# Chunked attention and a maxout layer on one core: units of 6, 8, 8 and 6 tiles, later transposes at the turn of two units, and another order of the free banks

## The chip, the cores and the metric

The kernel runs on one core of a Trainium2 chip. The metric is the device time of one execution in microseconds (us); the median of several runs counts.

## The reference

Attention inside chunks of 64 positions for 8 batches and 8 heads, then a layer that takes the largest of three products and projects it:

```python
scores = scale * np.matmul(q_c, k_c.transpose(0, 1, 2, 4, 3))     # chunks of 64 positions, heads of 64
scores = scores - np.max(scores, axis=-1, keepdims=True)
attn = np.exp(scores)
attn = attn / (np.sum(attn, axis=-1, keepdims=True) + 1e-09)
out = np.matmul(attn, v_c)
...
x = np.ascontiguousarray(attn_out.transpose(0, 2, 1, 3)).reshape(B * S, H * D)     # 4608 x 512
h = np.maximum(np.maximum(x @ w1, x @ w2), x @ w3)                                 # 4608 x 768
return (h @ w_out).astype(np.float32)                                              # 4608 x 512
```

## The kernel before, in words

The 4608 positions are 36 tiles of 128. The first eight tiles are two groups of four; the other 28 are four *units*, before of 8, 8, 6 and 6 tiles (`UNITS`, L27). A product of fp32 numbers is made of three matmuls on a high and a low part (`three`, L188 to L191), so nearly all of PE's work has the lines L189, L190 and L191.

*First group* (`first_group`, L642): an order written out by hand (`FIRST`, L49). It splits the weights into high and low parts, computes the attention of tiles 0 to 7 and the layer for tiles 0 to 3. Its last steps are the four output tiles, copied out of their banks at L360.

*Group 1* (tiles 4 to 7): its hidden part, 18 products of four steps each, and its projection (`project`, L364). Between the steps stand the attention steps of the first unit's tiles, one tile at a time (`tiles`, L703), and the sums of weights that the units need (`store`, L384), which go to DRAM.

*Units*: a unit's hidden part is nine *sets* of seven products (`hidden`, L490), a scheme that forms sums of weight blocks and of `X` blocks so that seven products do the work of eight; a product takes two steps of three matmuls, 512 columns wide in a unit of eight tiles and 384 in one of six. The weights of a set come from DRAM in two loads, 0.79 and 1.05 MB, into one of two buffers (`ring`, L471). After its nine sets a unit's tiles are projected (`project`, L574): the first four of six blocks for tiles 0 to 2, then the other two for them, then tile by tile; a tile's sum stays in one bank until ACT has copied it out (L564). While a unit is projected, the `X` operands of the next unit are made of `stage` (`operands`, L465: casts on ACT at L459, subtractions on DVE at L454 and L463, two of them on POOL).

*Attention of a tile* (`plain_steps`, L219): S, the scores (L239), in one half of the two banks of `s`; mx and sub, maximum and subtraction on DVE (L244, L249); exp on ACT (L253); sum, eps, rec on DVE (L197, L200, L203); nrm, the norm (L206); T, four transposes on PE (L262) into `tp`; at, the copy of `tp` on ACT (L267); V, the value product (L278); x, the copy into `stage` on ACT (L292 for single tiles, L726 for pairs). For the first unit's tiles V writes the other half of the same two banks of `s`. The tiles of later units are taken in pairs while the unit before runs: an *insertion* (`insertion`, L730) computes V of one pair, in two banks taken from the common ones, and S of the next, and plans the other steps of that next pair behind it.

The order is that of a planner: `plan(at, pe, fn)` puts a step on a list with a due time, and `passed(step)` (L666) advances the planned time by each PE step and issues what has come due, on whichever engine. Within an engine this order is the order of execution. `TABLE`, `PAIR` and `PAIR_T` (L32 to L37) hold the due times, `series` (L751) spreads a unit's insertions over its hidden part, the last one 3.5 us of planned time before its end.

Five banks serve all products of group 1 and the units. `take` hands out the first of a list, `give` puts a bank back at its end. In the first group a bank goes to the end of the list as soon as it is taken (`kept_until_read` is false), so group 1 begins with the banks in the order in which they were last taken.

Of the kernel before, what the change touches and what calls it, by code (L numbers as in the profile page):

```python
# [23 lines left out]
CT, JT = DM // P, DF // P  # L24
SCALE = 1.0 / float(D) ** 0.5
GROUPS = [4, 4]
UNITS = [8, 8, 6, 6]  # L27
HALF = 512
STEP, TILE = 0.6815, 2.05
STEP_H = {6: 0.517, 7: 0.6003, 8: 0.6815}  # L30
# [37 lines left out]
def chunk_attn_maxout_kernel(  # L68
# [27 lines left out]
    ps_m = ctx.enter_context(tc.tile_pool(name="ps_m", bufs=1, space=PSUM))  # L96
# [2 lines left out]
    first_x = tc.tile_pool(name="ps_x", bufs=1, space=PSUM)  # L99
    ps["ps_x"] = first_x.__enter__()  # L100

    banks, kept_until_read = [(ps_m, f"pm{n}") for n in range(3)], False

    def take():
        assert banks, "no bank is free"
        pool, tag = place = banks.pop(0)
        if not kept_until_read:
            banks.append(place)
        return pool.tile([P, 512], F32, name="pm", tag=tag), place

    def give(place):
        assert kept_until_read
        banks.append(place)
# [15 lines left out]
    for name in FIRST.split():  # L129
        k = (3 * int(name[1]) + int(name[2])) if name[0] in "WAXY" else None  # L130
# [57 lines left out]
    def three(o, ah, al, bh, bl, first, last):  # L188
        nc.tensor.matmul(out=o, lhsT=al, rhs=bh, start=first, stop=False)  # L189
        nc.tensor.matmul(out=o, lhsT=ah, rhs=bl, start=False, stop=False)  # L190
        nc.tensor.matmul(out=o, lhsT=ah, rhs=bh, start=False, stop=last)  # L191
# [117 lines left out]
    def moe(t0, x_of, first=False):  # L309


        hh, hl = [None] * JT, [None] * JT
        banks, ps, at = {}, {}, {}

        def bank(key):
            ps[key], at[key] = take()

        def read(key):
            if not first:
                give(at[key])  # L320


        def products(j, w, lo, hi):
            n, cols = hi - lo, slice(lo, hi)
            xh, xl = x_of()
            bank((j, w, lo))
            for ct in range(CT):
                three(ps[j, w, lo][:, :n], wh[j][:, w, ct, :], wl[j][:, w, ct, :], xh[:, ct, cols], xl[:, ct, cols],
                      ct == 0, ct == CT - 1)
                yield  # L330

        def maximum(j, w, lo, hi):
            n = hi - lo
            if w == 0:
                banks[j] = mp.tile([P, 512], F32, name="m")
                nc.scalar.copy(out=banks[j][:, :n], in_=ps[j, w, lo][:, :n])
            else:
                nc.vector.tensor_tensor(out=banks[j][:, :n], in0=ps[j, w, lo][:, :n], in1=banks[j][:, :n], op=ALU.max)
            read((j, w, lo))

        def high(j, lo, hi):
            if hh[j] is None:
                both = hpool.tile([P, 2, 512], F32R, name="h", tag=f"h{j}")
                hh[j], hl[j] = both[:, 0], both[:, 1]
            nc.scalar.copy(out=hh[j][:, lo:hi], in_=banks[j][:, :hi - lo])

        def low(j, lo, hi, eng=nc.vector):
            eng.tensor_tensor(out=hl[j][:, lo:hi], in0=banks[j][:, :hi - lo], in1=hh[j][:, lo:hi].bitcast(F32),
                              op=ALU.subtract)

        def onto(tt, j):
            if j == 0:
                bank(tt)
            cols = slice(tt * P, (tt + 1) * P)
            three(ps[tt], hh[j][:, cols], hl[j][:, cols], woh[:, j, :], wol[:, j, :], j == 0, j == JT - 1)

        def output(tt):
            outputs.append(tt)
            o = ao_p.tile([P, DO], F32, name="ao", tag=f"ao{len(outputs) % 4}")
            nc.scalar.copy(out=o, in_=ps[tt])  # L360
            read(tt)
            nc.sync.dma_start(out=out[(t0 + tt) * P:(t0 + tt + 1) * P, :], in_=o)

        def project(*tts, before=JT - 1):  # L364

            for js in (range(before), range(before, JT)):
                for tt in tts:
                    for j in js:
                        onto(tt, j)
                        yield [(0.3, lambda tt=tt: output(tt))] if j == JT - 1 else []  # L370

        def hidden(j, w):
            for ct, _ in enumerate(products(j, w, 0, 512)):
                yield [] if ct < CT - 1 else [(0.3, lambda: maximum(j, w, 0, 512))] + (
                [(1.1, lambda: high(j, 0, 512)), (1.8, lambda: low(j, 0, 512))] if w == 2 else [])

        return dict(products=products, maximum=maximum, high=high, low=low, hidden=hidden, project=project,
                    onto=onto, output=output)
# [295 lines left out]
    def plan(at, pe, fn):  # L674
        heapq.heappush(due, (at, len(order), pe, fn))
        order.append(fn)
# [21 lines left out]
    units, t0 = [], sum(GROUPS)  # L698
    for count in UNITS:
        units.append((unit(t0, count, rooms), t0, count))  # L700
        t0 += count

    def tiles(lead, time):  # L703
        _, t0, count = units[0]
        for tt in range(count):
            first = now + lead + (time - 13.5 - lead) * tt / (count - 1)
            for at, pe, fn in attention(t0 + tt, stage, tt * P, nc.vector, LATER):
                plan(first + at, pe, fn)
# [8 lines left out]
    def value_banks(both):  # L717
        def fn():
            both["banks"] = [take() for _ in range(2)]
            both["x"] = [p.rearrange("p (s g x) -> p s g x", s=2, g=4) for p, _ in both["banks"]]  # L720
        return fn

    def staged(both, c):
        def fn():
            to = stage()[:, :, both["col"]:both["col"] + 2 * P].rearrange("p g (s c x) -> p c s g x", s=2, c=2)
            nc.scalar.copy(out=to[:, c], in_=both["x"][c])  # L726
            give(both["banks"][c][1])
        return fn

    def insertion(when, k):  # L730

        scored = pairs[k]["tiles"] if k < len(pairs) else []
        if k:
            plan(when, 0.0, value_banks(pairs[k - 1]))
            for n, steps in enumerate(pairs[k - 1]["tiles"]):
                plan(when + 0.001 * (n + 1), 0.5, steps["V"])
                plan(when + 1.2 + 0.6 * n, 0.0, staged(pairs[k - 1], n))
        lead = 1.0 * bool(k)
        for n, steps in enumerate(scored):
            plan(when + 0.003 + 0.001 * n, 0.65, steps["S"])  # L740
            for name, *at in PAIR:
                fn = steps[name]
                plan(when + lead + at[n], 0.0, (lambda fn=fn: fn(nc.gpsimd)) if name == "nrm" else fn)
            for name, *at, pe in PAIR_T:
                plan(when + lead + at[n], pe, steps[name])
            plan(when + 6.0 + n, 0.0, steps["v"])
        if k + 1 < len(pairs):
            for n, steps in enumerate(pairs[k + 1]["tiles"]):
                plan(when + 4.0 + n, 0.0, steps["q"])

    def series(u, time):  # L751

        done = sum(count // 2 for _, _, count in units[1:u + 1])
        if u + 1 >= len(units):
            return
        n = units[u + 1][2] // 2
        lead = 9.0
        if u == 0:
            for m, steps in enumerate(pairs[0]["tiles"]):
                plan(now - 4.0 + m, 0.0, steps["q"])  # L760
            plan_at = now + 4.0
            insertion(plan_at, 0)
            lead = 20.0
        for k in range(n):
            insertion(now + lead + (time - 3.5 - lead) * k / (n - 1), done + k + 1)

    def stores():
        for n in range(len(sets)):
# [19 lines left out]

    inner = 3 * JT * CT * STEP + UNITS[0] * TILE
    parts += [("do", lambda: tiles(7.0, inner - 2.0))]  # L790
# [3 lines left out]
    def units_of(u):  # L794
        return UNITS[u] if u < len(UNITS) else 0

    for u, (it, t0, count) in enumerate(units):
        time = len(sets) * 14 * STEP_H[count] + (units_of(u + 1) * 1.6)
# [7 lines left out]
    now = -10.0  # L806
# [6 lines left out]
    with tc.manual_schedule(engines={ET.PE, ET.DVE, ET.Activation, ET.Pool, ET.SP}):  # L813
        first_group()
        kept_until_read = True
        for what, make in parts:
            if what == "do":
                make()
                continue
            for after in make():  # L820
                step, after = after if isinstance(after, tuple) else (STEP, after)
                for at, fn in after:
                    plan(now + step + at, 0.0, fn)
                passed(step)
        while due:
            heapq.heappop(due)[3]()
# [31 lines left out]
```

## Time and profile before

| | us |
|---|---|
| median of 3 runs (lowest, highest) | 670.89 (669.76, 671.49) |
| the profiled execution | 669.72 |
| its span, first to last instruction | 667.7 |
| busy in it: PE matmuls | 631.5 |
| PE weight loads | 536.1 |
| DVE | 416.1 |
| ACT | 233.4 |
| POOL | 210.5 |
| mean granted clock of TensorE | 0.985 of full |

PE's matmuls run one behind another; its weight loads lie beside them. An engine works through its own instructions in order, and an instruction that waits holds up all behind it on that engine. The profile names for each wait the instruction that ended it; "issue" stands where it names none. Times in the rows below are counted from the first instruction.

### The profile page before, as it was taken

The page shows a single profiled execution, that of the slowest core. Times are in us where ns is not written, and L with a number is a line of the kernel's source. Part 1 is how long each engine was busy: PE and PEld are TensorE (multiplying, and loading weights), DVE is VectorE, ACT ScalarE, POOL GpSimd, SP SyncE. Part 2 cuts the span into 40 slices and gives each one's busy share as a digit, 9 for nine tenths or more (in the row PEclk, how much of TensorE's full clock was granted, in tenths as well). Part 3 has the DMA queues.
Part 4 walks back from the last instruction along what each step waited for, and adds up shares of the span by engine and source line. Part 5 has one row for each costly group of instructions (what it writes and reads, how often), then busy time and mean ns, then how long its engine had stood idle before and what let it go on. Part 6 is the DMA issues. An engine that isn't in the chain of part 4 may idle for free.

```text
span 667.7 us, 12398 instructions
## 1 busy us (share of the span) xinstructions
PE 631.5 (95%) x5102; PEld 536.1 (80%) x5102; DVE 416.1 (62%) x663; ACT 233.4 (35%) x400; POOL 210.5 (32%) x184
## 2 busy tenths in 40 slices
PE   8899999787999999995999999969999999999997
PEld 4778868566788888884888888847999998999986
DVE  5889845576576967779027685790176867275640
ACT  5887633243442423244122223232132424121221
POOL 3324476563034232415012341340132322123210
PEclk9999999898999999997999999998999999999999
DMA  8979557364475756625217465162186636276502
GB/s 331 379 254 335 180 211 285 125 236 178 160 255 200 303 219 221 206 100 216 94 55 293 170 257 214 45 278 80 48 316 231 243 130 254 77 273 245 221 10 86
DMA packets 36055, 133.70 MB, mean 200 GB/s; under 512 B 4000, under 2 KB 6560, under 8 KB 30240
## 3 DMA queue, kind: packets, MB, share of 16 engines
q1 hardware_dynamic: 35856, 132.79, 53.9%
q8 instruction: 40, 0.66, 0.4%
q10 hardware_dynamic: 144, 0.13, 0.1%
q14 instruction: 15, 0.12, 0.1%
HBM read 106.95 MB, written 25.95 MB: 199 GB/s over the span
## 4 chain that ended last, share of the span: by engine, by line
PE 82%; DVE 10%; issue 2%; ACT 2%; POOL 2%; DMA 1%; SPq 0%; POOLq 0%; DVEq 0%; ACTq 0%
PE pm L189 25%; PE pm L190 25%; PE pm L191 25%; PE tp L262 2%; PE s L239 2%; PE pm L278 1%; DVE kept L454 1%; DVE X L463 1%; PE s L278 1%; DVE e L249 1%; DVE mx L244 1%; POOL kept L454 1%; DVE sm L197 1%; DVE H L533 1%; DMA buf<-in_qk 1%
## 5 line engine op out<-in xcount | busy, mean ns | idle before, releaser
L189 PE MATMUL pm<-X,ring 128*128 128x512 f32 (+1 forms) x504 | 185.0, 367 | 0.0
L190 PE MATMUL pm<-X,ring 128*128 128x512 f32 (+1 forms) x504 | 182.5, 362 | 0.0
L191 PE MATMUL pm<-X,ring 128*128 128x512 f32 (+1 forms) x504 | 182.5, 362 | 0.0
L511 DVE TENSOR_TENSOR kept<-pm,kept 128x512 f32<-128x512 f32 (+1 forms) x72 | 44.7, 621 | 122.9 <-PE pm L191 122.7
L517 POOL TENSOR_TENSOR kept<-kept 128x512 f32<-128x512 f32 (+1 forms) x36 | 41.4, 1151 | 246.4 <-DVE kept L511 233.2
L189 PEld LDWEIGHTS pm<-X,ring 128*128 128x128 f32 x504 | 94.6, 188 | 10.2 <-DVE pm L514 0.3
L191 PEld LDWEIGHTS pm<-X,ring 128*128 128x128 f32 x504 | 94.6, 188 | 10.2
L190 PEld LDWEIGHTS pm<-X,ring 128*128 128x128 f32 x504 | 94.7, 188 | 9.3
L508 ACT COPY kept<-pm 128x512 f32<-128x512 f32 (+1 forms) x72 | 38.4, 533 | 140.3 <-PE pm L191 134.8
L189 PE MATMUL pm<-woh,H 128*128 128x512 f32 x168 | 67.7, 403 | 0.0
L190 PE MATMUL pm<-wol,H 128*128 128x512 f32 x168 | 66.9, 398 | 0.0
L191 PE MATMUL pm<-woh,H 128*128 128x512 f32 x168 | 66.8, 398 | 0.0
L189 PE MATMUL pm<-xh,wl 128*128 128x512 f32 (+1 forms) x156 | 62.2, 399 | 1.7 <-ACT ao L360 1.7
L190 PE MATMUL pm<-xl,wh 128*128 128x512 f32 (+1 forms) x156 | 59.5, 381 | 0.3 <-DVE xl L289 0.3
L191 PE MATMUL pm<-xh,wh 128*128 128x512 f32 (+1 forms) x156 | 59.3, 380 | 0.0
L514 DVE TENSOR_TENSOR pm<-pm,kept 128x512 f32<-128x512 f32 (+1 forms) x72 | 45.3, 629 | 13.2 <-PE pm L191 12.6
L206 POOL TENSOR_TENSOR e<-e,sm 128x512 f32<-128x512 f32 x25 | 27.8, 1112 | 71.4 <-DVE sm L203 62.2
L523 DVE TENSOR_TENSOR most<-pm,most 128x512 f32<-128x512 f32 (+1 forms) x72 | 44.9, 623 | 2.1
L529 ACT CAST H<-most 128x512 fp32r<-128x512 f32 (+1 forms) x48 | 27.0, 569 | 37.9 <-DVE most L523 37.9
L244 DVE TENSOR_REDUCE mx<-s 128x8 f32<-128x512 f32 x36 | 24.6, 684 | 22.6 <-PE s L239 22.6
L262 PE MATMUL tp<-ident,e 128*128 128x128 f32 x144 | 23.0, 284 | 16.3 <-ACT xs L267 12.3
L189 PEld LDWEIGHTS pm<-woh,H 128*128 128x128 f32 x168 | 32.7, 195 | 6.8
(94 smaller groups left out, 961.7 us busy)
## 6 DMA issues: line engine op xcount, KB each, us to landing
ring<-w SPq DMA_DIRECT2D x36, 1024.0 KB, 6.7
ring<-w SPq DMA_DIRECT2D x36, 768.0 KB, 4.5
buf<-in_qk SPq DMA_DIRECT2D x36, 512.0 KB, 6.0
buf<-in_vb SPq DMA_DIRECT2D x36, 256.0 KB, 6.2
w<-s SPq DMA_DIRECT2D x9, 1024.0 KB, 5.1
out_x<-ao SPq DMA_DIRECT2D x35, 256.0 KB, 2.0
stage<-in_w SPq DMA_DIRECT2D x7, 512.0 KB, 5.4
xl<-in_w SPq DMA_DIRECT2D x5, 512.0 KB, 7.7
```

The lines of the kernel that those rows point to most:

```text
L189: nc.tensor.matmul(out=o, lhsT=al, rhs=bh, start=first, stop=False)
L190: nc.tensor.matmul(out=o, lhsT=ah, rhs=bl, start=False, stop=False)
L191: nc.tensor.matmul(out=o, lhsT=ah, rhs=bh, start=False, stop=last)
L206: eng.tensor_tensor(out=e, in0=e, in1=sm.unsqueeze(2).broadcast_to([P, 8, 64]), op=ALU.mult)
L244: nc.vector.tensor_reduce(out=st["mx"].rearrange("p (g c) -> p c g", c=2), in_=st["s"], axis=AX.X, op=ALU.max)
L262: nc.tensor.transpose(out=tp[:, g, :], in_=st["e"][:, g].rearrange("p c k -> p (c k)"), identity=ident)
L508: return lambda: nc.scalar.copy(out=kept(k), in_=o[i])
L511: return lambda: nc.vector.tensor_tensor(out=kept(k), in0=o[i], in1=kept(q), op=plus)
L514: return lambda: nc.vector.tensor_tensor(out=o[i] if w else M(j, c), in0=o[i], in1=kept(k), op=plus)
L517: nc.gpsimd.tensor_tensor(out=kept(2), in0=kept(2), in1=kept(1), op=plus)
L523: return lambda: nc.vector.tensor_tensor(out=M(j, c), in0=of(), in1=M(j, c), op=most)
L529: nc.scalar.copy(out=hh[j][:, c * half:(c + 1) * half], in_=M(j, c))
```

## The change

The units become 6, 8, 8 and 6 tiles. So six instead of eight single tiles stand in group 1, and 11 instead of 10 pairs in the units. `insertion` gets a time `behind`, by which the transposes of the pair that it scores, and their copies, stand later: 14 us of planned time for the last insertion of a unit's hidden part, 0 for the others. In the last but one unit the last insertion scores no pair. When the first group is done, the list of free banks is sorted by the place of each bank's last reading in the first group.

```diff
-UNITS = [8, 8, 6, 6]
+UNITS = [6, 8, 8, 6]
...
-    banks, kept_until_read = [(ps_m, f"pm{n}") for n in range(3)], False
+    banks, kept_until_read, read_last = [(ps_m, f"pm{n}") for n in range(3)], False, []
...
         def read(key):
-            if not first:
+            if first:
+                read_last.append(at[key])
+            else:
                 give(at[key])
...
-    def insertion(when, k):
+    def insertion(when, k, behind=0.0):
...
             for name, *at, pe in PAIR_T:
-                plan(when + lead + at[n], pe, steps[name])
+                plan(when + lead + behind + at[n], pe, steps[name])
...
         for k in range(n):
-            insertion(now + lead + (time - 3.5 - lead) * k / (n - 1), done + k + 1)
+            insertion(now + lead + (time - 3.5 - lead) * k / (n - 1), done + k + 1, 14.0 if k == n - 1 else 0.0)
...
         kept_until_read = True
+        banks.sort(key=lambda place: max(n for n, other in enumerate(read_last) if other == place))
```

What it moves, at two places. The first is PE's order in the hidden part of group 1. Before, one piece of it (`s<-buf` are the scores of a tile, `s<-xs,buf` the value product of the tile two ahead, `pm<-xh,wl` and the like the products of group 1):

```order
L190 MATMUL pm<-xl,wh_116 128x512
L191 MATMUL pm<-xh,wh_116 128x512
L239 MATMUL s<-buf 64x64 x16
L278 MATMUL s<-xs,buf 64x64 x16
L189 MATMUL pm<-xh,wl_122 128x512
L190 MATMUL pm<-xl,wh_116 128x512
```

and now:

```order
L278 MATMUL s<-xs,buf 64x64 x16
L189 MATMUL pm<-xh,wl_123 128x512
L190 MATMUL pm<-xl,wh_117 128x512
L191 MATMUL pm<-xh,wh_117 128x512
L189 MATMUL pm<-xh,wl_123 128x512
L190 MATMUL pm<-xl,wh_117 128x512
L191 MATMUL pm<-xh,wh_117 128x512
L239 MATMUL s<-buf 64x64 x16
L189 MATMUL pm<-xh,wl_123 128x512
L190 MATMUL pm<-xl,wh_117 128x512
L191 MATMUL pm<-xh,wh_117 128x512
```

Scores and value product no longer stand side by side: six matmuls of group 1 lie between a value product and the next scores, and 18 more, with a transpose after the first three, between those scores and the next value product.

The second is the projection of unit 0 on ACT. Before (`X` are the casts of the next unit's operands, `xs<-tp` the copies out of the transposes, `ao<-pm` the output tiles):

```order
L459 CAST X6_2135<-kept_2107 128x1024
L459 CAST X3_2141<-stage_1531 128x1024
L267 COPY xs_3385<-tp_3375 128x512
L459 CAST X7_2151<-stage_1531 128x1024
L459 CAST X4_2167<-kept_2107 128x1024
L267 COPY xs_3404<-tp_3395 128x512
L564 COPY ao_3413<-pm_3301 128x512
L564 COPY ao_3422<-pm_3344 128x512
```

and now:

```order
L461 CAST X3_2033<-stage_1512 128x1024
L461 CAST X7_2043<-stage_1512 128x1024
L461 CAST X4_2059<-kept_1999 128x1024
L566 COPY ao_3291<-pm_3193 128x512
L566 COPY ao_3300<-pm_3236 128x512
L566 COPY ao_3310<-pm_3261 128x512
L566 COPY ao_3332<-pm_3306 128x512
L566 COPY ao_3355<-pm_3328 128x512
L267 COPY xs_3362<-tp_3350 128x512
L267 COPY xs_3378<-tp_3370 128x512
L566 COPY ao_3390<-pm_3358 128x512
```

The two copies stood among the casts and now stand behind the outputs of five of the unit's six tiles; on PE the two transposes moved from behind the 9th and the 12th step of the projection to behind the 30th and the 33rd.

## Rows read from the trace of the kernel before

**Rows 1.** The page: busy time of PE; GB/s moved in 40 slices of the span.

```profile
PE 631.5 (95%) x5102; PEld 536.1 (80%) x5102; DVE 416.1 (62%) x663; ACT 233.4 (35%) x400; POOL 210.5 (32%) x184
GB/s 331 379 254 335 180 211 285 125 236 178 160 255 200 303 219 221 206 100 216 94 55 293 170 257 214 45 278 80 48 316 231 243 130 254 77 273 245 221 10 86
```

**Rows 2.** PE's waits, whole span: who waited for whom, us, times, longest.

```profile
PE s L278 <- issue: 8.4, 5, 3.0
...
PE s L278 <- ACT s L412: 2.6, 1, 2.6
PE pm L189 <- ACT ao L360: 1.7, 1, 1.7
```

**Rows 3.** Stretches: us, busy PE, PEld, DVE, ACT, POOL, clock, DMA share, GB/s.

```profile
97.95:177.68 79.73, 68.72 (x760) 54.32 (x761) 48.38 (x72) 27.73 (x43) 38.17 (x41) 0.96 0.55 197
...
294.48:338.37 43.89, 36.34 (x153) 29.50 (x152) 23.83 (x25) 14.69 (x21) 9.15 (x4) 0.92 0.42 162
...
432.60:475.76 43.16, 36.37 (x159) 29.48 (x153) 18.84 (x24) 12.87 (x21) 8.10 (x4) 0.92 0.40 161
475.76:549.21 73.45, 73.42 (x716) 71.83 (x714) 48.92 (x96) 20.32 (x40) 22.16 (x22) 1.00 0.57 209
549.21:573.86 24.65, 24.65 (x114) 20.37 (x109) 13.91 (x15) 10.39 (x17) 4.72 (x2) 1.00 0.52 202
573.86:639.41 65.55, 65.55 (x380) 65.54 (x378) 38.92 (x74) 13.64 (x28) 18.13 (x18) 1.00 0.54 201
```

**Rows 4.** The same view of four stretches at half clock.

```profile
121.75:124.90 3.15, 3.15 (x37) 2.65 (x38) 0.79 (x2) 1.11 (x2) 1.64 (x2) 0.50 0.29 83
155.40:159.00 3.60, 3.60 (x16) 2.80 (x10) 3.31 (x6) 1.70 (x3) 1.42 (x2) 0.53 0.50 182
311.02:316.10 5.08, 5.08 (x14) 4.20 (x15) 5.08 (x4) 1.85 (x3) 3.28 (x1) 0.50 0.02 3
451.26:456.00 4.74, 4.74 (x14) 3.87 (x15) 0.36 (x1) 2.00 (x4) 0.00 (x0) 0.50 0.29 111
```

**Rows 5.** Timelines of DVE, PE and ACT in group 1: start, us, instruction.

```profile
154.00 0.68 DVE L244 TENSOR_REDUCE mx<-s 128x8 f32<-128x512 f32 x1
...
154.79 0.69 PE L278 MATMUL s<-xs,buf 64*64 64x64 f32 x32 [2.60 <-ACT s L412]
...
163.35 0.69 PE L278 MATMUL s<-xs,buf 64*64 64x64 f32 x32 [0.87 <-issue]
...
175.56 0.69 PE L278 MATMUL s<-xs,buf 64*64 64x64 f32 x32
...
176.32 0.59 ACT L292 COPY stage<-s 128x512 f32<-128x512 f32 x1 [2.84 <-PE s L278]
```

**Rows 6.** PE's waits from 290 to 470 us, the two projections.

```profile
PE tp L262 <- ACT xs L267: 12.3, 2, 6.6
PE tp L262 <- POOL e L206: 2.0, 2, 1.1
```

**Rows 7.** ACT's timeline in the projections of units 0 and 1.

```profile
310.30 0.58 ACT L267 COPY xs<-tp 128x512 f32<-128x512 f32 x1
...
315.06 1.04 ACT L459 CAST X<-kept 128x1024 fp32r<-128x1024 f32 x1 [3.23 <-POOL kept L454]
...
449.80 0.83 ACT L459 CAST X<-kept 128x768 fp32r<-128x768 f32 x1 [3.63 <-POOL kept L454]
```

**Rows 8.** DVE: one row of unit 0's projection; two groups by shape (count, busy us, mean ns).

```profile
305.04 0.68 DVE L533 TENSOR_TENSOR H<-most,H 128x512 fp32r<-128x512 f32 x1
...
L523 DVE TENSOR_TENSOR most<-pm,most 128x512 f32<-128x512 f32 x36 | 24.9, 690 | 1.0
...
L523 DVE TENSOR_TENSOR most<-pm,most 128x384 f32<-128x384 f32 x36 | 20.0, 556 | 1.1
```

**Rows 9.** The chain that ended last, in group 1: start, us, what.

```profile
169.53 0.62 PE s L278 x32
```

**Rows 10.** DMA issued at 493.14: KB, us from issue to landing.

```profile
ring<-w SPq DMA_DIRECT2D x1, 1024.0 KB, 8.2
```

## The prediction

> **What bounds the kernel now.** I read the page's busy times first, then PE's list of waits, then the span cut into the program's stages, and last the timelines around each wait. PE works for 631.5 of 667.7 us [rows 1], and no other engine comes near that, so the end moves only with PE's idle time, its slow-clock time, or its work. The work stays: units of 6, 8, 8 and 6 hold the products of 8, 8, 6 and 6. So the sum is made of PE's waits and of what the clock takes behind them. In the list of waits the reader is to see three places [rows 2, 6]: a first product of group 1 that waited 1.7 us for a bank still being copied out, six value products (L278) of group 1 that waited 8.4 + 2.6 = 11.0 us, and the transposes (L262) of the pair scored last in units 0 and 1, which waited 12.3 + 2.0 = 14.3 us. With some idle time in the first 25 us, which nothing here touches, that is all.
>
> **The clock.** Behind four of these waits the granted clock stood at half, 1.2 GHz, for a while [rows 4]: 3.15 and 3.6 us in group 1, 5.08 and 4.74 us in the two projections. PE was busy all through them, so half of each is lost: 1.6 + 1.7 = 3.3 us in group 1 (the second stretch is at 0.53, so 0.47 x 3.6), and 2.5 + 2.4 = 4.9 us at the transposes. It rose again by itself each time. I count this as part of the price of the wait ahead of it, so that it goes with the wait.
>
> **Free banks in order of last reading.** The first product of group 1 now takes a bank that was read before the last output copies, and the copy that ended its wait (L360) is one of three in a row. Worth 1.7 us; between 0, if another of the three is still met, and 1.7. I take 1.7: the next product comes four steps of 0.68 us later (24.65 us for 36 steps of a projection [rows 3]), longer than the copies last.
>
> **Six tiles instead of eight in group 1.** In [rows 5] the maximum of a tile runs on DVE from 154.00 to 154.68 us, and the value product starts at 154.79: it waits for the maximum of the tile two ahead, because scores and values lie in halves of the same two banks and stand side by side in PE's order. The profile puts it down to an ACT cast, and names nothing for the other five, but all six end like that, 0.1 us behind a maximum. In the new order 24 matmuls (5.5 us) and a transpose lie between one score product and the next, and of these 18 stand ahead of the value product, 4.1 us behind the scores: maximum and subtraction (0.7 us each) are long done. So the 11.0 us go, with 3.3 us of slow clock: 14.3 us. What is late next is the score product, six matmuls behind a value product. It needs the copy out of the other half. In [rows 5] a value product starts at 175.56 and its copy ends at 176.91, 1.35 us later; PE comes to the scores after 0.62 [rows 9] + 6 x 0.228 = 1.99 us (0.228 is 24.65 us over the 108 matmuls of a projection of six tiles). That leaves 0.6 us if ACT is free; behind a cast of 1.04 us [rows 7] some 0.4 us are missing. I take 0.5 us in all, for one such meeting; the bounds are 0 and 4 us (a whole cast for each of four tiles).
>
> The Trainium skill (PSUM — Partial Sum Buffer, Terms) counts it as an error when TensorE and another engine touch one bank in the same quadrant at once. By that rule every sharing of the two banks still waits after the change, and the sum would be that of the second rival below, 641.7 us. The trace bears out the waiting for DVE in six of six cases; that ACT is late at the score product no row shows.
>
> **Two tiles scored as a pair instead.** The three insertions of unit 2 make its hidden part longer than that of unit 3, which has none: (73.45 - 65.55) / 3 = 2.6 us for the products and transposes of two tiles [rows 3]. Two single tiles have four products of 0.62 us [rows 9], 2.5 us, and two transposes besides. So it is some 0.5 us less at best; I take 0. Their place is unit 1, with an insertion every 29 us of the plan.
>
> **The late transposes, units 0 and 1.** Both were held by ACT: in [rows 7] the copy out of the first transpose (L267) ran at 310.30, behind casts of the next unit's operands that wait for DVE and POOL, and the second transpose began at 311.02, 6.6 us late. Now the transposes stand 30 steps or more into the projection, over 20 us after its start, and their copies on ACT behind all those casts and five output copies; the value products that need them come 9 us into the next unit. Both waits (14.3 us) go with their 4.9 us of clock. What is late next:
> - *The low part of hidden block 5 for the first tiles (L533).* The 14th step of the projection needs it. Before, it was done at 305.7 [rows 8], and PE, not held by transposes, would have come to it at 294.48 + 13 x 0.685 = 303.4: 2.3 us were hidden. With unit 0 of six tiles ten DVE instructions ahead of it work on 384 columns, 0.556 instead of 0.690 us [rows 8], which brings it 1.3 us forward: 1.0 us of waiting remains (0 to 2.3, if none of it comes forward). At the end of unit 1 the scores stand behind the last hidden product and the block is done before them: 0.
> - *The sixth accumulator.* PE has five banks and begins the sixth tile's projection after 30 steps, 20.5 us. Its bank is the first tile's, copied out behind the last operand cast: 315.06 + 1.04 [rows 7] and a copy of 0.59 [rows 5] make 316.7 before, 22.2 us after the projection's start. In unit 0 less 1.3 us as above that is 20.9, against 20.5 + 1.0 for PE: 0. Behind unit 1 the last cast stood at 449.80 + 0.83 [rows 7], 18.0 us after the projection's start at 432.6, for six-tile operands; eight-tile ones lengthen some eight DVE steps by 0.27 us (256 columns, twice the difference in [rows 8]): 20.1 + 0.6, against 20.5. I take 0.5 (0 to 3).
>
> **A denser unit 0.** Its hidden part takes 65.55 us plus five insertions of 2.6 us, 78.7 us [rows 3]. DVE: 38.92 us without attention, and (48.92 - 38.92) / 2 = 5.0 us for each pair scored, so 38.9 + 25 = 64 of 78.7 us. DMA: nine sets of 1.84 MB, six pairs of q and k at 1.05 MB and five of v at 0.52 MB are 25.4 MB, 323 GB/s, where a slice of this run reached 379 [rows 1]. Neither is full, but both bunch up, so 0.5 us (0 to 5).
>
> **The sum.** 1.7 + 14.3 + 14.3 + 4.9 = 35.2 us go, 0.5 + 1.0 + 0.5 + 0.5 = 2.5 us come: 32.7 us less. The profiled execution took 669.72 us (span 667.68 and 2.04 around it), so 637.0; the median of the runs stands 1.17 us above that execution, so **638.2 us**. With all new waits at 0 it is 635.7, and a sum of the stages in place of the waits (each of them free of waits) comes 1 us lower still. With the bounds 4 + 2.3 + 3 + 5 instead of 2.5 it would be 650; that all meet their upper end I don't believe.
>
> **Rivals.**
> - *The projection's wait comes back as another.* If the operand chain (DVE, POOL, ACT by turns) lasts 3 us longer than I worked out, the sixth accumulator waits some 3.5 us at each of two projections, and half clock costs 1.6 us each, as behind the 3.0 us wait in group 1: 10.2 us in place of 1.5, so 647 us. For it speaks that ACT's copies stand behind that chain; against it that DVE gets less work there, not more. Chance 0.12.
> - *The wait in group 1 passes from the value product to the scores.* Each score product there finds ACT still busy for a whole cast of 1.04 us ahead of the copy it needs: 4 us in place of 0.5, 641.7 us, as by the bank rule above. For it: the two still share the banks; against it: 0.6 us of room. Chance 0.06.
> - *DVE sets the pace of group 1.* Two value products in [rows 5] are 163.35 - 154.79 = 8.6 us apart; I expect 24 x 0.228 + 2 x 0.62 and a transpose, some 7.4 us. If 8.6 is DVE's own pace, five intervals give back 6 us, as waits of the transposes for the norm, in place of the 0.5: 643.7 us. Against it: DVE was busy for 48.4 of 79.7 us [rows 3]. Chance 0.11.
> - *Slower: unit 0 waits for its weights.* A set of six tiles lasts 7.28 us, and the set's second load must land within that and one product of 1.04 us, 8.3 us; the latest such load in unit 2, beside a pair's tiles, landed 8.2 us after its issue [rows 10]. Nothing is in reserve. Unit 0 would have pairs' loads beside more of its sets. If the nine loads land 12 to 13 us after issue, PE loses about 4.5 us a set, 40 us, and it is 638 + 40 = 678 us; from 3.6 us a set (32.7 / 9) the change is slower than before. Against it: the mean rate asked for is under what was reached. Chance 0.05, of which 0.03 slower and 0.02 about the same.
> - *Nothing at the bank.* If the wait of 1.7 us at L360 is not one for the bank taken first, it stays: 639.9 us; this lies within my forecast.
>
> **How the numbers follow.** The forecast has 0.66 (its own range 634 to 642). Range 633.5 to 647: at the bottom the sum of stages and a little more, at the top the first rival. About 0.3%, 2 us, is what a measurement of this kernel can tell from no change. Faster 0.95, same 0.02, slower 0.03: only the rival on unit 0 reaches the last two.
>
> **What would show it.** Right: no wait of L278 in group 1, whose hidden part takes 62 to 64 us instead of 79.73 [rows 3]; no L262 wait over 1 us behind units 0 and 1; the clock at full from there to the end; a projection of unit 0 of 25 to 27 us. Wrong: PE waiting for L533 or for an output copy for over 2 us, DMA of the ring among what PE waits for in unit 0, or new waits of L239 for the copy out of `s`.

## The result and the profile after

The changed kernel took 638.13 us (median of 4 runs, 637.23 to 639.75) against 671.02 us (4 runs, 669.76 to 671.49): a ratio of 0.9515, 95% interval 0.949 to 0.954. The forecast was 638.2. The profiled execution took 637.51 us with a span of 635.7, 32.0 us less than the span before.

First the page: busy time by engine, and the clock that TensorE was granted in 40 slices of the span. The answer to [rows 1] is 8.3 us less of PE's time, about what the four stretches of [rows 4] had cost (3.3 + 4.9), and a clock of 9 (90% or more) in every slice.

```profile
PE 623.2 (98%) x5101; PEld 530.0 (83%) x5102; DVE 415.0 (65%) x661; ACT 233.9 (37%) x400; POOL 217.9 (34%) x186
...
PEclk9999999999999999999999999999999999999999
```

PE's waits from 30 us on, all of them (who waited for whom, us in total, times, longest). L278 and L262 of [rows 2, 6] are gone, and so is L189 behind an output copy of the first group. Two of the five below are those that the prediction named as late next.

```profile
PE pm L189 <- DVE H L535: 1.4, 1, 1.4
PE pm L189 <- ACT ao L566: 1.1, 1, 1.1
PE s L239 <- issue: 1.1, 1, 1.1
PE pm L189 <- DVE most L525: 0.3, 1, 0.3
PE pm L189 <- DMA ring<-w: 0.2, 1, 0.2
```

(L535, L525 and L566 are L533, L523 and L564 of the kernel before.) The stages, with the columns of [rows 3]: hidden part of group 1, then hidden part and projection of units 0, 1 and 2.

```profile
95.64:157.75 62.11, 62.11 (x626) 48.65 (x624) 44.57 (x60) 26.24 (x40) 41.26 (x42) 1.00 0.66 240
...
174.07:256.02 81.95, 80.42 (x987) 77.56 (x986) 56.28 (x116) 27.58 (x54) 26.54 (x26) 1.00 0.69 245
256.02:283.15 27.13, 25.78 (x118) 20.96 (x117) 22.81 (x25) 12.64 (x19) 8.96 (x4) 1.00 0.62 242
283.15:380.66 97.51, 97.51 (x915) 80.73 (x913) 64.91 (x108) 28.35 (x49) 29.27 (x24) 1.00 0.52 185
380.66:415.82 35.16, 34.06 (x159) 27.85 (x153) 22.39 (x24) 14.20 (x21) 10.32 (x4) 1.00 0.50 199
415.82:509.12 93.30, 93.30 (x716) 77.13 (x714) 60.03 (x96) 23.82 (x41) 27.24 (x22) 1.00 0.45 164
509.12:541.89 32.77, 32.77 (x150) 27.14 (x145) 14.44 (x15) 11.47 (x18) 7.96 (x2) 1.00 0.43 168
```

Read them by the first and second number: where length and busy time of PE are equal, nothing waits. That holds for all but unit 0 and the two projections behind units 0 and 1. A unit of 6 tiles can't be set against one of 8, so the stages are added up by kind (hidden parts of the units of before are 100.48, 94.23, 73.45 and 65.55; the stretches not shown come from the same view):

| us of the profiled execution | before | after | forecast of the difference | measured |
|---|---|---|---|---|
| all that stands ahead of group 1 | 97.95 | 95.64 | -1.7 | -2.3 |
| group 1 hidden, two tiles fewer | 79.73 | 62.11 | | -17.6 |
| four hidden parts, two tiles more | 333.71 | 338.34 | | +4.6 |
| group 1 and hidden parts together | 413.44 | 400.45 | -14.3 + 0.5 + 0.5 | -13.0 |
| the four projections ahead of the last | 128.02 | 111.38 | -19.2 + 1.0 + 0.5 | -16.6 |

The terms sum to -32.7 and the measured rows to -31.9.

The timeline in group 1 shows what replaced [rows 5] (start, us, instruction). From one score product to the next it is 8.3 us here, with 27 matmuls of group 1 between them; in the other intervals that hold a value product it is 7.6 us with 24 matmuls or 8.3 with 27. PE waits in none of them, so this is PE's own pace.

```profile
134.43 0.69 PE L239 MATMUL s<-buf 64*64 64x64 f32 x32
...
135.26 0.69 DVE L244 TENSOR_REDUCE mx<-s 128x8 f32<-128x512 f32 x1 [0.78 <-PE s L239]
...
137.28 0.68 DVE L249 TENSOR_TENSOR e<-s,mx 128x512 f32<-128x512 f32 x1
...
140.53 0.69 PE L278 MATMUL s<-xs,buf 64*64 64x64 f32 x32
...
141.29 0.59 ACT L292 COPY stage<-s 128x512 f32<-128x512 f32 x1 [0.31 <-PE s L278]
...
142.75 0.69 PE L239 MATMUL s<-buf 64*64 64x64 f32 x32
```

Maximum and subtraction are done 2.6 us ahead of the value product, and the copy ends at 141.88, 0.87 us ahead of the next scores, where 0.6 us of room had been worked out.

### The profile page after: what moved, and what is told of

Its sections match the earlier page's. It is cut to its first block, busy times and chain, and to the rows that moved or that the text cites. A ratio compares the mean times of both kernels' runs of the same rounds, so it can differ in the third digit from the quotient of the medians.

```text
span 635.7 us, 12387 instructions
## 1 busy us (share of the span) xinstructions
PE 623.2 (98%) x5101; PEld 530.0 (83%) x5102; DVE 415.0 (65%) x661; ACT 233.9 (37%) x400; POOL 217.9 (34%) x186
## 4 chain that ended last, share of the span: by engine, by line
PE 88%; DVE 8%; DMA 1%; POOL 1%; issue 1%; ACT 1%; SPq 0%; ACTq 0%; POOLq 0%; DVEq 0%
PE pm L189 27%; PE pm L190 26%; PE pm L191 26%; PE s L239 3%; PE tp L262 2%; PE pm L278 2%; DMA ring<-w 1%; PE s L278 1%; DVE X L465 1%; DVE most L525 1%; PE pm L638 1%; DVE e L249 1%; DVE sm L197 1%; DVE mx L244 1%; DVE kept L456 1%
## 5 line engine op out<-in xcount | busy, mean ns | idle before, releaser
L189 PE MATMUL pm<-X,ring 128*128 128x512 f32 (+1 forms) x504 | 185.4, 368 | 0.5 <-DVE most L525 0.3
L519 POOL TENSOR_TENSOR kept<-kept 128x384 f32<-128x384 f32 (+1 forms) x36 | 41.5, 1152 | 229.1 <-DVE kept L513 218.8
L513 DVE TENSOR_TENSOR kept<-pm,kept 128x384 f32<-128x384 f32 (+1 forms) x72 | 44.8, 622 | 110.6 <-PE pm L191 109.9
L189 PEld LDWEIGHTS pm<-X,ring 128*128 128x128 f32 x504 | 94.6, 188 | 11.5 <-DVE most L525 1.1
L510 ACT COPY kept<-pm 128x384 f32<-128x384 f32 (+1 forms) x72 | 38.4, 533 | 124.0 <-PE pm L191 116.8
L189 PE MATMUL pm<-woh,H 128*128 128x512 f32 x168 | 66.2, 394 | 2.5 <-DVE H L535 1.4
L190 PE MATMUL pm<-wol,H 128*128 128x512 f32 x168 | 65.5, 390 | 0.0
L191 PE MATMUL pm<-woh,H 128*128 128x512 f32 x168 | 65.5, 390 | 0.0
L189 PE MATMUL pm<-xh,wl 128*128 128x512 f32 (+1 forms) x156 | 61.0, 391 | 0.0
L206 POOL TENSOR_TENSOR e<-e,sm 128x512 f32<-128x512 f32 x27 | 30.3, 1124 | 74.4 <-DVE sm L203 73.6
L516 DVE TENSOR_TENSOR pm<-pm,kept 128x384 f32<-128x384 f32 (+1 forms) x72 | 45.3, 629 | 14.3 <-PE pm L191 14.1
L525 DVE TENSOR_TENSOR most<-pm,most 128x384 f32<-128x384 f32 (+1 forms) x72 | 44.9, 624 | 2.1
L531 ACT CAST H<-most 128x384 fp32r<-128x384 f32 (+1 forms) x48 | 27.0, 568 | 40.7 <-DVE most L525 40.7
L189 PEld LDWEIGHTS pm<-woh,H 128*128 128x128 f32 x168 | 31.5, 188 | 9.7 <-DVE H L535 1.8
L191 PEld LDWEIGHTS pm<-woh,H 128*128 128x128 f32 x168 | 31.5, 188 | 6.7
```

Source lines behind the costliest of these rows:

```text
L206: eng.tensor_tensor(out=e, in0=e, in1=sm.unsqueeze(2).broadcast_to([P, 8, 64]), op=ALU.mult)
L510: return lambda: nc.scalar.copy(out=kept(k), in_=o[i])
L513: return lambda: nc.vector.tensor_tensor(out=kept(k), in0=o[i], in1=kept(q), op=plus)
L516: return lambda: nc.vector.tensor_tensor(out=o[i] if w else M(j, c), in0=o[i], in1=kept(k), op=plus)
L519: nc.gpsimd.tensor_tensor(out=kept(2), in0=kept(2), in1=kept(1), op=plus)
L525: return lambda: nc.vector.tensor_tensor(out=M(j, c), in0=of(), in1=M(j, c), op=most)
```

## The experiments

The kernel before ran beside them on the same chips: 670.5 us beside E1 to E4, 670.9 beside E5 to E8, 670.0 beside E9 to E12. Ratios are to it, with 95% intervals.

**E1 to E4: each part alone, and the mechanism in group 1.**

E1 puts the units back:

```diff
-UNITS = [6, 8, 8, 6]
+UNITS = [8, 8, 6, 6]
```

> The changed kernel with its units put back to 8, 8, 6 and 6; late transposes and bank order stay. Theory (the prediction's terms add up): group 1 takes its 11.0 us of waiting and 3.3 us of slow clock back, 14.3 us, less the 0.5 us that I had put on new waits and with 1 us more for L533, whose instructions then work on 512 columns: 638.1 + 14.3 + 0.5 = some 653 us, hidden part of group 1 near 79.7 us again. Rival (the order of the units also carries the gain at the late transposes, because operands of six tiles are cast earlier): over 658 us, with L262 waiting behind units 0 and 1.

Measured: 654.25 us, 0.9753 (0.9723 to 0.9783), so 16 us come back. PE's waits from 30 us on, and group 1 with its first slow stretch:

```profile
PE s L278 <- issue: 8.3, 5, 3.0
PE s L278 <- ACT s L414: 2.6, 1, 2.6
PE pm L189 <- DVE H L535: 2.3, 1, 2.3
```

```profile
96.48:178.90 82.42, 71.49 (x761) 56.45 (x760) 48.34 (x72) 29.47 (x46) 39.97 (x42) 0.92 0.55 200
119.50:126.33 6.83, 6.18 (x46) 5.12 (x47) 2.98 (x6) 1.73 (x4) 2.29 (x2) 0.50 0.59 186
```

The six waits are those of [rows 2] to within 0.1 us. No L262 stands there, so the late transposes don't need the order of the units. L535 waits 2.3 us with eight tiles in unit 0, the upper bound that the prediction gave for just this case. Group 1 is 2.7 us longer than before at equal waits: three stretches at half clock instead of two, the first of them 6.8 us.

E2 takes the move of the transposes out:

```diff
-..., 14.0 if k == n - 1 else 0.0)
+..., 0.0)
```

> The changed kernel without the 14 us by which the last pair's transposes stand later; units and bank order stay. Theory: the transposes wait for their copies behind the operand casts again, 14.3 us and 4.9 us of half clock, less the waits at L533 and L566 that PE then no longer meets (2.5 us): 638.1 + 16.7 = 654.8 us. Rival (with units of 6, 8, 8, 6 the operands come early enough and the move does nothing): 638 to 641 us.

Measured: 656.59 us, 0.9786 (0.9745 to 0.9827), 18.5 us back. Its waits, and the two projections with the slow stretch in the first:

```profile
PE tp L262 <- ACT xs L267: 12.4, 2, 6.2
PE tp L262 <- POOL e L206: 2.4, 2, 2.2
PE s L239 <- issue: 2.0, 1, 2.0
```

```profile
256.39:291.37 34.98, 28.53 (x118) 22.91 (x117) 22.74 (x25) 12.68 (x19) 8.89 (x4) 0.90 0.48 188
271.00:277.60 6.60, 5.69 (x16) 4.66 (x17) 6.60 (x4) 3.37 (x6) 3.76 (x2) 0.51 0.01 3
388.88:434.49 45.61, 37.27 (x159) 30.32 (x153) 22.30 (x24) 14.38 (x21) 10.23 (x4) 0.89 0.38 153
```

The rival falls: with six tiles the operands come no earlier in a way that helps. The two projections are 18.3 us longer than those of the changed kernel, which is the whole difference. 14.8 of it are waits, and 6.0 more are busy time of PE, which the stretches at half clock draw out; the 2.5 us of waits at L535 and L566 are gone, as expected.

E3 is the kernel before with one edit:

```diff
-LATER = {..., "V": 2.8, "x": 2.8}
+LATER = {..., "V": 2.3, "x": 2.3}
```

> The kernel before, 8 tiles in group 1, with one edit: value products and their copies stand 0.5 us earlier in the table, so that a value product, still right behind the scores of the tile two ahead on PE, is written ahead of that tile's maximum and no longer after it. Theory A (the program's own order makes the wait: a value product written after the maximum waits for a semaphore of DVE, since both touch the tile s): the six waits and their slow clock go with eight tiles too, 671.0 - 14.3 = 656.7 us, hidden part of group 1 near 65.4 us, and the maximum waits for the value product instead. Theory B (the prediction's: it is enough that scores and values stand side by side in halves of the same banks): the waits stay, 671 us. Between them, 660 to 668, if the wait passes on to the scores or transposes behind.

Measured: 659.53 us, 0.9847 (0.9809 to 0.9886), hidden part of group 1 71.79 us. What the edit does to the program of PE (rows of its order with the semaphores that they wait for; first before, then E3):

```
509 L239 MATMUL s<-buf 64x64 [waits DMAHW5_49,DVE_49]
511 L278 MATMUL s<-xs,buf 64x64 [waits DMAHW4_49,DVE_49,Activation_49]

509 L239 MATMUL s<-buf 64x64 [waits DMAHW5_49,DVE_49]
511 L278 MATMUL s<-xs,buf 64x64 [waits DMAHW4_49,Activation_49]
```

The place on PE is the same, right behind the scores; only the wait on DVE has gone, since the value product is now written ahead of the maximum. So theory B falls: standing side by side was not enough for the wait. Theory A holds for the waits of the value product on the maximum, but not for the whole time, as 4.9 us of new waits are left:

```profile
PE s L239 <- DVE e L249: 2.7, 2, 1.4
PE s L278 <- ACT xs L267: 2.2, 3, 0.9
```

The timeline shows where the first kind comes from:

```profile
130.82 0.70 PE L239 MATMUL s<-buf 64*64 64x64 f32 x32
...
131.33 0.65 PE L278 MATMUL s<-xs,buf 64*64 64x64 f32 x32
...
136.06 0.68 DVE L244 TENSOR_REDUCE mx<-s 128x8 f32<-128x512 f32 x1
...
136.78 0.58 ACT L292 COPY stage<-s 128x512 f32<-128x512 f32 x1 [1.71 <-DVE mx L244]
...
137.40 0.69 DVE L249 TENSOR_TENSOR e<-s,mx 128x512 f32<-128x512 f32 x1 [0.65 <-ACT stage L292]
...
138.14 0.69 PE L239 MATMUL s<-buf 64*64 64x64 f32 x32 [1.39 <-DVE e L249]
```

DVE comes to the maximum 4.5 us behind the scores' end, after its other work; the copy on ACT, which only reads the other half, waits for the maximum; the subtraction waits for the copy; the next scores wait for the subtraction. Here all that touches `s` goes one after the other, in the order in which it is written. The second kind is a value product that waits for the copy of its transpose; in two of the three cases that copy stands on ACT behind the exp and a copy that were late with this chain, in the third behind an exp alone.

The Trainium skill (PSUM — Partial Sum Buffer, PSUM bank collisions raise a hardware error) gives the reason for such semaphores: two engines must not be on one bank and quadrant at once, two readers included. The copy's 1.71 us behind a maximum of other columns agree with that.

E4 is the changed kernel, six tiles, with the value products moved behind scores and maximum of the tile two ahead:

```diff
-LATER = {..., "V": 2.8, "x": 2.8}
+LATER = {..., "V": 4.9, "x": 4.9}
...
-            first = now + lead + (time - 13.5 - lead) * tt / (count - 1)
+            first = now + lead + (time - 16.5 - lead) * tt / (count - 1)
```

> The changed kernel, six tiles in group 1, with the value products put behind the scores of the tile two ahead and behind that tile's maximum in the program (tiles 0.6 us closer, values 2.1 us later). Theory A and B of the run before alike: the waits come back with six tiles, one with PE right behind the scores (1.7 us) and three with a product of 0.68 us between (1.0 us each), 4.7 us, and up to 1.6 us of slow clock: 643 to 645 us. Rival (six tiles alone take the wait away, because DVE is less loaded): 638 us.

Measured: 641.74 us, 0.9567 (0.9533 to 0.9601), hidden part of group 1 65.39 us, 3.3 more than in the changed kernel. Two rows of its waits, then the longest one, which again ended 0.1 us behind a maximum on DVE, whatever the profile puts it down to:

```profile
PE s L278 <- ACT m L338: 3.1, 2, 2.2
...
PE s L278 <- ACT h L347: 0.3, 1, 0.3
```

```profile
143.40 0.68 DVE L244 TENSOR_REDUCE mx<-s 128x8 f32<-128x512 f32 x1
...
144.19 0.69 PE L278 MATMUL s<-xs,buf 64*64 64x64 f32 x32 [2.25 <-ACT m L338]
```

So the wait comes back with six tiles where the place in the table asks for it, 3.6 us in all instead of the 4.7 expected, and in the profiled run without slow clock.

**E5 to E8: the bank, the distance, the order, and the waits that are left.**

E5 leaves out the line that sorts the banks.

> The changed kernel without the line that sorts the free banks; units and late transposes stay. Theory: the first product of group 1 gets a bank that an output copy still reads and waits 1.7 us again, 638.1 + 1.7 = 639.8 us, with L189 waiting for ao L362 ahead of group 1 in PE's waits. Rival (the sort takes no wait away, since the other banks are as late): 638.1 us and no such wait in either.

Measured: 640.6 us, 0.957 (0.9534 to 0.9605). The trace has the wait, as in [rows 2]:

```profile
PE pm L189 <- ACT ao L362: 1.7, 1, 1.7
```

By the times alone it couldn't be told: the interval overlaps that of the changed kernel.

E6 moves the transposes by half as much:

```diff
-..., 14.0 if k == n - 1 else 0.0)
+..., 7.0 if k == n - 1 else 0.0)
```

> The changed kernel with the last pair's transposes 7 us later in the table in place of 14. Theory (the second transpose waits for the copy of the first, and that copy for the last operand cast on ACT): casts end 20.7 us into the projection of unit 0 and 21.3 us into that of unit 1, and the second transpose is asked for some 17.5 and 19.5 us in, so it waits 3.7 us and 2.4 us, the first wait for L535 stays, that for the sixth accumulator goes: 638.1 + 6.1 - 1.1 + up to 3 of half clock = 643 to 646 us. Rival (any move behind the last hidden maxima is enough, the norm on POOL being what was late): 638 us.

Measured: 650.64 us, 0.9708 (0.9676 to 0.974). Half of the distance brings a third of the gain. The projection of unit 0, ACT and PE:

```profile
273.64 1.04 ACT L461 CAST X<-kept 128x1024 fp32r<-128x1024 f32 x1 [3.38 <-POOL kept L456]
...
274.59 1.55 ACT L566 COPY ao<-pm 128x512 f32<-128x512 f32 x3
...
276.02 0.61 ACT L267 COPY xs<-tp 128x512 f32<-128x512 f32 x1
...
276.77 1.09 PE L262 MATMUL tp<-ident,e 128*128 128x128 f32 x4 [4.75 <-ACT xs L267]
```

The theory is right in kind, but the waits are 4.75 and 4.84 us in place of 3.7 and 2.4, mainly because it left out the three output copies (1.55 us) that stand between the last cast and the copy of the first transpose. The half clock behind the waits cost more too: PE is busy in the two projections for 4.75 us longer than in the changed kernel (28.15 + 36.44 against 25.78 + 34.06 us), where up to 3 were expected. In the changed kernel the first transpose runs at 278.11, its copy at 279.82 and the second at 280.64, without a wait, and the last cast has ended at 276.71. That copy ends 0.2 us ahead of the second transpose: the 14 us hold hardly any reserve there.

E7 is the changed kernel with units of 8, 8, 6 and 6 again and E3's edit.

> Units back to 8, 8, 6 and 6, late transposes and bank order kept, and the value products of group 1 written ahead of the maximum. Theory: the value products' waits stay away without the new order of units; what was left of them in group 1 of the run with that edit alone (hidden part 71.8 us) stays: that run's 659.5 less 14.3 + 4.9 - 2.3 (L535) for the transposes and 1.7 for the bank = 641 us. If this is at 638 or below, the new order of units was not needed; if it is at 645 or above, the chain of the tile s (copy, maximum, subtraction by turns on ACT and DVE) is worth more with eight tiles than that run showed.

Measured: 642.94 us, 0.9593 (0.9565 to 0.9621), group 1:

```profile
94.81:166.48 71.67, 66.80 (x761) 52.85 (x760) 49.33 (x72) 29.18 (x46) 40.02 (x42) 0.98 0.64 230
```

So half a microsecond in the table would have brought 11.3 of the 16.1 us that the new units bring (E1 against E7 and against the changed kernel). What is left is mainly the 4.9 us of waits that E3 has too; no run tried to take them away with eight tiles.

E8 tries the two waits that the changed kernel has left:

```diff
-(8.4, high(4)), (9.4, low(4))]
+(16.0, high(4)), (17.0, low(4))]
...
-        parts += [("steps", lambda it=it: it["project"](0, 1, 2, before=4))]
-        parts += [("steps", lambda it=it, tt=tt: it["project"](tt)) for tt in range(3, count)]
+        parts += [("steps", lambda it=it: it["project"](0, 1, 2, 3, before=4))]
+        parts += [("steps", lambda it=it, tt=tt: it["project"](tt)) for tt in range(4, count)]
```

> The changed kernel with two more edits at the places where it still waits: the projection of a unit takes its first four tiles (not three) through hidden blocks 0 to 3 before it asks for block 5, which comes 2.7 us later so; and the cast of the seventh operand stands behind three output copies on ACT. Theory (the waits of 1.35 us at L535 and 1.1 us at L566 are what the rows name): both go, 638.1 - 2.45 = 635.7 us. Rival (the sixth accumulator then waits for its copy, which comes four steps later): no gain, 638 us or more, with L566 among PE's waits at both projections.

Measured: 635.58 us, 0.9486 (0.9457 to 0.9516), with neither wait in the trace.

**E9 to E12: the better version beside the changed kernel.** The changed kernel again, each edit of E8 alone (E10 the projection, E11 the cast), and both.

> The changed kernel as it is, beside the three others on one chip: 638 us, waits of 1.35 us at L535 and 1.1 us at L566, and somewhere from 0 to 2 us in the scores of unit 0 with no wait named.

> The changed kernel with four tiles in place of three ahead of block 5 in a unit's projection. Theory: the wait at L535 goes (1.35 us), that at L566 stays (1.1 us or more, the copy being asked for later): 636.8 us. Rival (the output copies, four steps later, hold up the sixth accumulator by more than that): 638 to 640 us.

> The changed kernel with the seventh operand's cast behind three output copies. Theory: the wait at L566 goes (1.1 us), that at L535 stays: 637.0 us. Rival (the low part of that operand, now later on DVE, or the room it is read from hold up the next unit's first products): 638 us or more, with L189 or L510 waiting at the start of a unit.

> Both edits again, beside the changed kernel on the same chip: 635.7 us, 0.996 of the changed kernel, no wait at L535 or L566.

| kernel | us, median of 6 | ratio (95%) | projections of units 0 and 1 |
|---|---|---|---|
| E9, changed | 637.14 | 0.9491 (0.9462 to 0.9519) | 27.15, 35.16 |
| E10, four tiles first | 637.70 | 0.9505 (0.9479 to 0.953) | 27.11, 35.17 |
| E11, late cast | 636.35 | 0.9487 (0.9462 to 0.9512) | 27.15, 33.76 |
| E12, both | 635.08 | 0.9474 (0.9449 to 0.9498) | 25.50, 33.76 |

E10 missed: L535 no longer waits, but unit 0's projection is no shorter. ACT's queue runs as in the changed kernel: the last cast ends 20.7 us into the projection and the copy of the first transpose begins 23.8 us in, in both. So PE, no longer held at L535, meets that queue: a bank comes 0.19 us late, the second transpose 0.97 us. Ahead of that copy ACT itself waits 0.69 us for a DMA to clear the buffer of an output tile. E10's waits, and ACT's:

```profile
PE pm L189 <- ACT ao L566: 1.3, 2, 1.1
PE tp L262 <- ACT xs L267: 1.0, 1, 1.0
```

```profile
277.23 0.59 ACT L566 COPY ao<-pm 128x512 f32<-128x512 f32 x1 [0.69 <-DMA out_x<-ao]
```

E11 hit: L566 no longer waits and unit 1's projection is 1.4 us shorter; no wait at the next unit's start took its place. With both edits L535 goes too. E12's two projections are free of waits, 3.0 us shorter than E9's together:

```profile
256.33:281.83 25.50, 25.50 (x117) 21.06 (x117) 22.83 (x25) 12.55 (x19) 8.98 (x4) 1.00 0.66 258
379.36:413.12 33.76, 33.76 (x158) 27.92 (x153) 22.38 (x24) 14.08 (x21) 10.32 (x4) 1.00 0.51 206
```

In time that is 2.1 us between medians, 0.3%; the intervals overlap, so the gain rests on the two traces of that version (E8 and E12) more than on the times. It is the fastest version here.

## Why the prediction was right

**The bank.** Right: E5 has the wait of 1.65 us back. The stage ahead of group 1 ended another 0.7 us earlier, but that start lies between 94.81 and 96.48 us in the runs that sort the banks, so this is no part of the change.

**Group 1.** The size is right: -17.6 us there and +3.3 us for a fourth pair in unit 1 (97.51 against 94.23) make the -14.3 forecast, and the undone order (E1) costs 16 us. The new waits of the scores, 0.5 us in the sum, came to none. The step "because scores and values lie in halves of the same two banks and stand side by side in PE's order" was incomplete: E3 has them side by side and the value product doesn't wait for the maximum. What makes that wait is that the value product was written behind the maximum. The conclusion survived because six tiles change this too: the value product then stands 2.2 us of the plan ahead of the scores of the tile two ahead, and E4 shows the wait back with six tiles behind the maximum.

**The late transposes.** Right in place, cause and size: E2 costs 18.5 us, where 16.7 were expected. E6 shows that it is ACT's queue, casts first and output copies behind them, that the transposes had to clear.

**What is late next.** Both places were named and both are there. L535 waited 1.35 us where 1.0 was taken, and with eight tiles 2.3, as worked out (E1). The sixth accumulator waited 1.1 us behind unit 1 where 0.5 was taken, and none behind unit 0, as forecast; that is twice what was taken, within the bounds of 0 to 3. With the wait at L535 the projection of unit 0 took 27.13 us, just over the 25 to 27 named as a sign of being right.

**Unit 0.** Its hidden part took 81.95 us where 78.7 was forecast, plus 0.5. Two parts of that. First the "2.6 us" for an insertion came from dividing by three, though one of the three scores no pair; a run without waits (E10) has 79.66, so the five cost 14.1 us and not 13.0. This doesn't touch the sum, since the same work is missing elsewhere. Then waits, 1.5 us named in the profile after: not the weights of the ring, from which 0.16 us came, but the 1.05 us in the scores (below). Here the term "a denser unit 0" was too small by about 1 us.

**The rivals.** No projection waited 3 us; the scores of group 1 didn't wait; DVE, busy for 44.6 of 62.1 us there, set no pace with six tiles; with eight, once the other wait is gone, its late maximum begins the chain of new waits (E3). Unit 0 waited 0.2 us for its weights (in E11, the most of all runs, 1.0 us), where the rival has 40. The sum came within 1 us since terms missed in both directions: -0.7 ahead of group 1 and -0.5 at the scores, +0.4, +0.6 and about +1 behind. That the median came within 0.1 us is luck besides: the profiled execution took 637.5 us where 637.0 was forecast, and the median stands 0.6 us above it, not the 1.17 us that were carried over from the kernel before.

## What to carry to other kernels

A PE wait that ends right behind another engine's reading of the same PSUM tile may be one that the program's own order asks for: look which of the two is written first before you change the load, since half a microsecond in a table (E3, E7) was worth some 70% of a new split of the work. When an instruction is moved out of a queue's way, it has to clear everything that stands in that queue, not only what held it (E6), and a wait that is taken away may come back at the next thing that the same queue holds up (E10). Price a wait together with the slow clock behind it: in the profile of the kernel before that was about a third on top (3.3 on 11.0 us, 4.9 on 14.3), but it varies (last section).

## What the runs showed of the hardware

**PE seems to have waited for its instructions.** In seven traces with six tiles in unit 0 PE stood still for 0.79 to 2.05 us inside the scores of a pair, 59 to 61 matmuls into 64, where no semaphore is waited for ("issue" in the profile). In all seven one packet of the instruction queue began shortly before and took 0.9 to 1.0 us, and the matmuls went on 2.2 to 2.4 us after its start. In three (E5, E6, E10) there was no wait, and the packet had begun 2.4, 4.8 and 5.0 us ahead of that matmul. First E9 (PE's timeline, and the instruction queue's packet that began in the tenth of a microsecond from 214.90 us), then E10 (the same, from 210.00 us):

```profile
214.50 1.09 PE L239 MATMUL s<-buf 64*64 64x64 f32 x59
217.33 0.34 PE L239 MATMUL s<-buf 64*64 64x64 f32 x5 [1.74 <-issue]
```

```profile
q8 instruction: 1, 0.02, 58.2%
```

```profile
214.24 1.11 PE L239 MATMUL s<-buf 64*64 64x64 f32 x64
```

```profile
q8 instruction: 1, 0.02, 104.2%
```

The hidden part of unit 0 is 79.7 to 80.0 us in the three and 81.5 to 82.7 in the seven, a difference of the size by which two runs of one kernel differ (634.85 to 638.29 us in E9). The packets are of 16 KB (40 of them, 0.66 MB, on the page of the profile after), and PE runs 10,203 instructions, 255 to a packet, so I take them for PE's own program; the pairs' products, many and short (64 matmuls and their weight loads in 1.1 us), use it up fastest. That the packet is late because the ring's loads keep the DMA engines full (82% of their time from 197.2 to 214.8 us in E9) is only argued: no run tried it, and over the same stretch they are full for 80% in E10, which has no wait. In the last 5 us ahead of the packet they are full for 97% in E9 and for 56% in E10.

The Trainium skill (Runtime: NRT & Kernel Launch, Instruction fetch mechanics) says that instructions come in blocks of 16 KiB and that crossing into the next is mostly hidden. The size agrees; if these packets are PE's program, it wasn't hidden in those seven traces.

**The clock's price is not fixed.** With the same six waits in group 1, before had two stretches at half clock, 1.2 GHz [rows 4], which cost 3.3 us, and E1 three, of 6.8, 3.4 and 3.4 us, which cost 6.5 us (half of PE's busy time in them). E4's waits, of up to 2.25 us, brought none in the profiled run, though two of its four runs have a mean granted clock of 0.997; E3's, of up to 1.4 us, brought one of 3.4 us. The profiled run of the kernel before was a mild one: its mean clock was 0.985, and 22 of the 25 runs of that kernel beside the experiments have 0.977 to 0.982.
